# Weight loads in smaller pieces and later, loads limited to three under way, and the first batch routed two steps earlier, in a fused attention and mixture-of-depths kernel

## The chip, the cores and the metric

The kernel runs on one core of a Trainium2 chip. The metric is the device time of one execution in microseconds. Before the change it is 194.29 us, the median of three runs (193.64 to 196.32). A profile of one execution shows a span of 191.8 us, from the first to the last instruction.

The engines of a core run their own instruction streams and meet through semaphores: PE (matrix products; "PEld" is its loading of weights), DVE (vector work), ACT (copies out of the matrix memory and activations), POOL (further elementwise work, and the DMAs with row indices) and SP (issues plain loads). Data comes and goes through 16 DMA engines.

## The reference

Two stages, in 32-bit floating point. The first is linear attention with a decay per head, for 4 batches, 8 heads, 768 positions and a head size of 64, in blocks of 64 positions:

```python
for b in range(nb):
    intra = np.einsum('bhic,bhjc->bhij', qb, kb) * Dmask[None]
    intra = np.einsum('bhij,bhjd->bhid', intra, vb)
    inter = np.einsum('bhid,bhde->bhie', qb * lam_pow[None], kv_state)
    out[:, :, sl] = intra + inter
    kb_dec = kb * rev_pow[None]
    kv_state = lam_block[None, :, None, None] * kv_state + np.einsum('bhsd,bhse->bhde', kb_dec, vb)
```

The heads' outputs side by side give x of 768 tokens by 512 for each batch. The second stage gives each token a score, picks the 128 tokens of a batch with the highest scores, and adds a gated two-layer network to those alone:

```python
scores = np.einsum('bsd,d->bs', x, w_gate)
for b in range(B):
    top_idx = np.argpartition(-scores[b], capacity)[:capacity]
    xe = x[b, top_idx]
    h = np.maximum(xe @ w1, 0.0)
    ye = h @ w2
    g = 1.0 / (1.0 + np.exp(-scores[b, top_idx]))
    out[b, top_idx] = x[b, top_idx] + g[:, None] * ye
```

w1 is 512 x 1024 and w2 is 1024 x 512, 2 MB each.

## The kernel before

A *group* is 128 positions of one batch with all eight heads: two blocks of the reference. There are six groups in a batch (NT = 6) and 24 in all (NG = 24). The main loop (line 620) runs over groups; its pass g is called step g. It finishes group g and prepares groups g+1 and g+2. The order of the instructions on each engine is the order in which the program writes them (`manual_schedule`), so what a step writes first runs first on its engine.

The parts of a step, with their lines:

- `transposes(g+2)` turns queries and keys on PE (lines 199 and 210), and ACT copies them out (202, 216 or 219).
- `queries_decayed` and `keys_decayed` multiply by powers of the decay on POOL (224 and 187), giving qs and kd.
- `scores(g+1)` (line 237, PE) and `masked(g+1)` (244, DVE) give the block's masked scores p. `from_states(g+1)` (297) adds the share of the earlier blocks' state, which needs qs. `from_scores(g)` (308) multiplies p by the values; `outputs(g)` copies the result to x_b on ACT (322, 324) and stores it (334).
- `state_products(g+2)` (260, PE) gives keys times values. `next_state` adds them to the decayed state on DVE: either the decay is done first on POOL (`decay_state`, 270) and added (287), or both are folded into four DVE instructions (282).
- `gate_scores(g)` (347, DVE) gives the scores of the group's tokens. `row(g-1)` (370, PE) turns them into a row, and `compare(g-1)` and `compare_older` (376, 386, DVE) count for each token how many beat it.

When a batch is complete, `plan` (546) sets the steps of its second stage. `ranks` (422, 427, DVE) turns the counts into a 0/1 matrix "hit". `tokens` (438 on PE, 444 and 447 on DVE) makes the list of chosen tokens. `fetch` (461, POOL) gathers their rows from the output in memory into xs. `gate` (471 to 486) transposes xs and computes the gates. Then come 16 pieces on PE: eight `hidden` (499), each one eighth of the first layer, with a relu on ACT (504) after every four, and eight `back` (513), each one eighth of the second layer. After the last, DVE computes y (521) and POOL writes the rows back with an indirect DMA (525). The pieces are dealt out over steps by `counts`, so that PE has work in each. For the first batch: hit in step 6, tokens and fetch in step 8, gate in step 9, and four pieces in each of steps 9 to 12. For the second: hit, tokens and fetch in step 13, gate and pieces from step 15. The third runs into the end of the loop, and the fourth comes after it.

There are two forms of a step. The form for the start ("spare", steps below `SPARE` = 9) puts the transposes of g+2 first and folds one of the two state updates. The other (from step 9) puts the transposes late, uses half of the state products' bank for the transposed keys and lets POOL decay both states.

Loads are all issued by SP in program order: q, k and v of a group as three DMAs of 256 KB (line 69; runs of 64 elements, 256 bytes), six steps ahead (`AHEAD` = 6), into a ring of seven buffers (`AHEAD + 1`). A load waits until its buffer's last reader is done; nothing else holds it back. The weights stand in the same queue: w1 as four DMAs of 512 KB with runs of 1024 elements (4 KB, line 88) in step 2, w2 as four of 512 KB with runs of 2 KB (line 91) in steps 4 to 7:

```python
weights_at = [NT // 2 - 1] * NDC + [NT // 2 + 1 + i for i in range(NFC // 2)]
for g in range(NG):
    if g + AHEAD < NG:
        load(g + AHEAD)
```

The x_b of the second batch is not stored group by group but kept, and stored as two DMAs of 768 KB from step 12 on.

## Time and profile before

| | |
|---|---|
| time, median of 3 | 194.29 us |
| span of the profiled execution | 191.8 us |
| PE busy | 156.0 us (81%) |
| DVE / POOL / ACT busy | 112.7 / 94.2 / 68.3 us |
| loads on SP's queue (q1) | 76,544 packets, 23.07 MB |
| stores on ACT's queue (q10) | 3,538 packets, 6.30 MB |
| instruction fetches (q8) | 28 packets, 0.46 MB |
| q, k and v loads, issue to landing, median | 5.7 to 5.8 us |
| gather of xs, issue to landing, median | 4.6 us |

Two parts of the page show the span in 40 slices of 4.8 us, one digit for each, in tenths (9 is 90% or more): PEclk is the clock that PE was granted, DMA the busy share of the DMA engines.

```profile
PEclk9999999999669955999999969999999999999997
DMA  5999997899899999999879999411013211011001
```

The DMA engines are busy for the first 25 slices, about 120 us, and nearly idle after that. The clock of PE falls in three places: around 50, around 70 and around 108 us. A mean over the whole span hides this, so the kernel has to be read stage by stage. In the views of instructions in order of time, a line gives start, duration, engine, source line, operation, tiles (out<-in) and count, and in brackets the idle time of the engine before it with what ended it; "issue" means that it waited for nothing that the profile shows.

### The profile page before, as it was taken

The page shows a single profiled execution, that of the slowest core. Times are in us where ns is not written, and L with a number is a line of the kernel's source. Part 1 is how long each engine was busy: PE and PEld are TensorE (multiplying, and loading weights), DVE is VectorE, ACT ScalarE, POOL GpSimd, SP SyncE. Part 2 cuts the span into 40 slices and gives each one's busy share as a digit, 9 for nine tenths or more (in the row PEclk, how much of TensorE's full clock was granted, in tenths as well). Part 3 has the DMA queues.
Part 4 walks back from the last instruction along what each step waited for, and adds up shares of the span by engine and source line. Part 5 has one row for each costly group of instructions (what it writes and reads, how often), then busy time and mean ns, then how long its engine had stood idle before and what let it go on. Part 6 is the DMA issues. An engine that isn't in the chain of part 4 may idle for free.

```text
span 191.8 us, 8134 instructions
## 1 busy us (share of the span) xinstructions
PE 156.0 (81%) x3522; PEld 126.2 (66%) x3522; DVE 112.7 (59%) x382; ACT 68.3 (36%) x175; POOL 94.2 (49%) x102
## 2 busy tenths in 40 slices
PE   0897768685497459999996299999998988989990
PEld 0566657574486359996755299998666977539730
DVE  3813578589547423437698558767966889620000
ACT  2234545544055103344425055546244634111100
POOL 3358656736154525057448777676777610021002
PEclk9999999999669955999999969999999999999997
DMA  5999997899899999999879999411013211011001
GB/s 112 224 218 213 235 257 198 210 313 305 212 241 233 260 255 269 213 190 211 267 240 279 274 219 220 114 60 58 6 55 113 113 58 58 0 55 55 3 0 55
DMA packets 80757, 31.99 MB, mean 167 GB/s; under 512 B 75601, under 2 KB 75601, under 8 KB 80722
## 3 DMA queue, kind: packets, MB, share of 16 engines
q1 hardware_dynamic: 76544, 23.07, 54.7%
q10 hardware_dynamic: 3538, 6.30, 9.0%
q0 software_dynamic: 640, 2.10, 3.2%
q8 instruction: 28, 0.46, 1.1%
q14 instruction: 7, 0.06, 0.1%
HBM read 24.12 MB, written 7.34 MB: 164 GB/s over the span
## 4 chain that ended last, share of the span: by engine, by line
PE 43%; issue 15%; DVE 11%; DMA 7%; POOL 6%; ACT 3%; POOLq 1%; ACTq 0%; DVEq 0%
PE ph L499 9%; PE py L513 7%; PE po L308 5%; PE tq L199 5%; PE po L237 4%; PE pu L260 4%; DMA out_dram<-y,tok 4%; PE po L297 4%; DMA xs<-out_dram,tok 3%; ACT qT L202 3%; DVE cmp L386 2%; POOL qs L224 2%; DVE xg L347 2%; PE pu L210 2%; POOL decayed L270 2%
## 5 line engine op out<-in xcount | busy, mean ns | idle before, releaser
L270 POOL TENSOR_TENSOR decayed<-state,decay 128x256 f32<-128x256 f32 x32 | 28.5, 890 | 27.4 <-DVE state L282 12.3
L224 POOL TENSOR_TENSOR qs<-qT,qpow 128x512 f32<-128x512 f32 x24 | 30.8, 1282 | 20.8 <-ACT qT L202 19.2
L499 PE MATMUL ph<-xsT,w_sb 128*128 128x128 f32 x256 | 32.1, 285 | 0.7 <-ACT xsT L475 0.7
L499 PEld LDWEIGHTS ph<-xsT,w_sb 128*128 128x128 f32 x256 | 30.9, 200 | 1.1 <-ACT xsT L475 0.9
L386 DVE TENSOR_SCALAR_CACHE_REDUCE cmp<-sc_row,sc 128x128 bf16<-128x128 f32 (+3 forms) x66 | 29.9, 498 | 0.0
L187 POOL TENSOR_TENSOR kd<-kn,kpow 128x512 f32<-128x512 f32 x24 | 25.9, 1080 | 7.1 <-DMA kn<-in_k_dram 4.0
L513 PE MATMUL py<-w_sb,hs 128*128 128x512 f32 x64 | 29.2, 597 | 0.2 <-ACT qT L202 0.2
L202 ACT COPY qT<-tq 128x512 f32<-128x512 f32 x24 | 14.0, 584 | 39.3 <-PE tq L199 36.0
L237 PE MATMUL po<-qT,kT 64*64 64x64 f32 x768 | 18.7, 232 | 7.1 <-issue 6.4
L347 DVE CUSTOM_DVE_ANT_0 xg<-x_b,wg_b 128x512 f32<-128x512 f32 x24 | 24.2, 1007 | 0.0
L244 DVE TENSOR_TENSOR p<-po,mask 128x512 f32<-128x512 f32 x24 | 16.5, 688 | 12.9 <-PE po L297 12.8
L260 PE MATMUL pu<-vn,kd 64*64 64x64 f32 x704 | 19.6, 233 | 3.3 <-DVE state L287 3.3
L199 PE MATMUL tq<-ident,qn 128*128 128x128 f32 x96 | 17.6, 312 | 4.9 <-DMA qn<-in_q_dram 4.9
L237 PEld LDWEIGHTS po<-qT,kT 64*64 64x64 f32 x768 | 15.9, 146 | 8.2 <-issue 7.1
L308 PE MATMUL po<-vn,p 64*64 64x64 f32 x768 | 18.2, 232 | 3.3 <-issue 3.0
L308 PEld LDWEIGHTS po<-vn,p 64*64 64x64 f32 x768 | 14.5, 141 | 9.1 <-issue 5.8
L287 DVE TENSOR_TENSOR state<-pu,decayed 128x256 f32<-128x256 f32 x32 | 13.5, 420 | 11.7 <-ACT kT L219 7.6
L297 PE MATMUL po<-state,qs 64*64 64x64 f32 x704 | 18.1, 230 | 2.7 <-issue 1.5
L260 PEld LDWEIGHTS pu<-vn,kd 64*64 64x64 f32 x704 | 16.9, 147 | 5.1 <-issue 2.9
L513 PEld LDWEIGHTS py<-w_sb,hs 128*128 128x128 f32 x64 | 11.5, 191 | 11.4 <-issue 11.0
L376 DVE SCALAR_TENSOR_TENSOR cmp<-pb,sc,not_before 128x128 bf16<-128x128 f32 x22 | 7.7, 348 | 19.3 <-ACT sc_row L373 11.2
L297 PEld LDWEIGHTS po<-state,qs 64*64 64x64 f32 x704 | 15.6, 145 | 3.5 <-issue 2.1
(66 smaller groups left out, 170.3 us busy)
## 6 DMA issues: line engine op xcount, KB each, us to landing
qn<-in_q_dram SPq DMA_DIRECT2D x24, 256.0 KB, 5.8
kn<-in_k_dram SPq DMA_DIRECT2D x24, 256.0 KB, 5.7
vn<-in_v_dram SPq DMA_DIRECT2D x24, 256.0 KB, 5.7
out_dram<-x_b ACTq DMA_DIRECT2D x18, 256.0 KB, 4.3
w_sb<-in_moe_w_dram SPq DMA_DIRECT2D x8, 512.0 KB, 5.9
out_dram<-x_b ACTq DMA_DIRECT2D x2, 768.0 KB, 5.6
xs<-out_dram,tok POOLq DMA_INDIRECT x4, 4.6
out_dram<-y,tok POOLq DMA_INDIRECT x4, 3.1
```

Source lines behind the costliest of these rows:

```text
L187: nc.gpsimd.tensor_tensor(out=kd[:], in0=loaded[g][1][:], in1=kpow[:].rearrange("p a b -> p (a b)").unsqueeze(2).broadcast_to([128, H, D]) ...
L199: nc.tensor.transpose(tq[:, hp, :], in_=loaded[g][0][:, 2 * hp : 2 * hp + 2, :], identity=ident[:])
L224: nc.gpsimd.tensor_tensor(out=qs[:], in0=qTs[g][:], in1=qpow[:].rearrange("p a c i -> p a (c i)"), op=ALU.mult)
L237: nc.tensor.matmul(po[half[c], hh, 1, hp, :], lhsT=kT[half[hh], hp, half[c]], rhs=qT[half[hh], hp, half[c]], start=True, stop=True, skip_g ...
L260: nc.tensor.matmul(us[g][c][half[hh], hp * D : (hp + 1) * D], lhsT=kd[half[c], h, :], rhs=vn[half[c], h, :], start=True, stop=True, skip_g ...
L270: nc.gpsimd.tensor_tensor(out=t[:], in0=states[n][:], in1=decay[:], op=ALU.mult)
L297: nc.tensor.matmul(pos[g][half[hh ^ c], hh, 0, hp, :], lhsT=qs[half[hh], hp, half[c]], rhs=states[n][half[hh], hp, :], start=(hp == 0), st ...
L308: nc.tensor.matmul(pos[g][half[hh ^ c], hh, 0, hp, :], lhsT=p[half[c], hh, hp, :], rhs=vn[half[c], 2 * hp + hh, :], start=(hp == 0 and (2 ...
L347: nc.vector.tensor_tensor_reduce(out=xg[:], in0=x_bs[b][:, t].rearrange("p a b e -> p (a b e)"), in1=wg_b[:], scale=1.0, scalar=0.0, op0=A ...
L386: nc.vector.tensor_scalar(out=cmp[:, : cols.stop - cols.start], in0=rows_[b][:, cols], scalar1=scs[b][:, t : t + 1], scalar2=None, op0=op, ...
L499: nc.tensor.matmul(ph[:, fc % 4, :], lhsT=w1_sb[:, dc, fc * 128 : (fc + 1) * 128], rhs=keep["xsT"][:, dc, :], start=(dc == 0), stop=(dc == ...
L513: nc.tensor.matmul(py[:], lhsT=keep["hs"][:, fc, :], rhs=w2_sb[:, fc, :], start=(fc == 0), stop=(fc == NFC - 1),)
```

## The change

It has several parts:

- **Loads under way.** All loads go through `fetch_in`, which makes each of the first 31 loads (those of groups 0 to 8 and w1) wait on SP for the landing of the third load before it.
- **Three steps ahead.** `AHEAD` becomes 3. The ring keeps its seven buffers, so SP may still run ahead of the steps; what moves is the place of a load in the program, and with it the order among loads and weights.
- **Weights.** w1 comes behind group 8, as four DMAs of 512 KB, each a quarter of the columns with runs of 256 elements (1 KB). w2 comes as eight DMAs of 256 KB with runs of 1 KB, four behind group 10 and four behind group 11.
- **First batch earlier.** Its hit, tokens and fetch all come in step 6, its gate in step 7, its pieces as 3, 3, 3, 3, 2, 2 in steps 7 to 12. Its counting of older groups becomes part of `compare` again.
- **A third form of a step** for steps 6 to 11 (`g < FED`): transposes late, pieces before them, one state update folded. The start's form ends with step 5 (`SPARE` = 6).
- **The write of y** becomes a piece of its own, at the end of the step after the last `back`: step 13 for the first batch and step 21 for the second.
- The kept x_b of the second batch is stored from step 11 on.

It is meant to keep the queue of loads short while PE needs instructions and gathers through the same DMA engines, to have the weights there no earlier than needed, to give PE pieces earlier, and to take POOL's wait for y away.

The core of the diff:

```diff
-    AHEAD = 6
-    SPARE = NT + 3
+    AHEAD = 3
+    SPARE = NT
+    FED = 2 * NT
...
-    ld = ctx.enter_context(tc.tile_pool(name="ld", bufs=AHEAD + 1))
+    ld = ctx.enter_context(tc.tile_pool(name="ld", bufs=7))
...
+    def fetch_in(out, in_):
+        dma = nc.sync.dma_start(out=out, in_=in_)
+        if 3 <= len(issued) < 3 * (NT + 3) + F // 256:
+            tc.add_manual_dep(
+                dma.ins, issued[-3].ins.name,
+                mybir.DependencyInfo(mybir.DependencyClass.Sync, mybir.DependencyReason.DATA),
+                reason="loads under way",
+            )
+        issued.append(dma)
...
     def load_weights(i):
-        if i < NDC:
-            nc.sync.dma_start(out=w1_sb[:, i, :], in_=moe_w1[i * 128 : (i + 1) * 128, :])
+        if i < F // 256:
+            c, j, n, dst, src = i, 0, NDC, w1_sb, moe_w1
         else:
...
+            j, c = divmod(i - F // 256, HD // 256)
+            j, n, dst, src = 2 * j, 2, w2_sb, moe_w2
+        cols = slice(c * 256, (c + 1) * 256)
+        fetch_in(
+            dst[:, j : j + n, cols],
+            src[j * 128 : (j + n) * 128, cols].rearrange("(c p) e -> p c e", p=128),
+        )
...
-                nc.gpsimd.indirect_dma_start(
-                    out=rows_upto(b), out_offset=rows_at(), in_=y[:], in_offset=None,
-                )
+                keep["y"] = y
...
+        def write():
+            nc.gpsimd.indirect_dma_start(
+                out=rows_upto(b), out_offset=rows_at(), in_=keep["y"][:], in_offset=None,
+            )
...
-            ranked[s + 1 if b > 0 else s] = ranks
-            put(s + 1 if b > 0 else s + 2, 25, tokens)
+            at = s + 1 if b > 0 else s
+            ranked[at] = ranks
+            put(at, 25, tokens)
...
-            put(s + 2 if first else s + 1, 26, fetch)
-            gates[s + 3] = gate
+            put(s if first else s + 1, 26, fetch)
+            gates[s + 1 if first else s + 3] = gate
...
-            counts = [1, 2] if not whole else [4, 4, 4, 4] if first else [2, 3, 3, 3, 3, 2]
+            counts = [1, 2] if not whole else [3, 3, 3, 3, 2, 2] if first else [2, 3, 3, 3, 3, 2]
...
+            if step + 1 < NG:
+                writes.setdefault(step + 1, []).append(write)
...
-    weights_at = [NT // 2 - 1] * NDC + [NT // 2 + 1 + i for i in range(NFC // 2)]
+    n_w1, n_w2 = F // 256, NFC * HD // 512
+    weights_at = [NT + 2 - AHEAD] * n_w1 + [
+        NT + 4 - AHEAD + 2 * i // n_w2 for i in range(n_w2)
+    ]
...
-        if g >= 2 * NT and kept:
+        if g >= 2 * NT - 1 and kept:
...
+        elif g < FED and g + 3 < NG:
+            if g == NT:
+                for r in rows:
+                    row(r)
+            decay_state(2 * g + 4)
+            from_scores(g)
+            outputs(g)
+            scores(g + 1)
+            from_states(g + 1)
+            keys_decayed(g + 2)
+            if g == NT:
+                for r in rows:
+                    compare(r)
+                if g in ranked:
+                    ranked.pop(g)()
+            masked(g + 1)
+            if g in gates:
+                gates.pop(g)()
+            if g > NT:
+                in_order(pieces)
+            gate_scores(g)
+            start_u(g + 2)
+            transposes(g + 2)
+            state_products(g + 2)
+            next_state(2 * g + 4)
+            queries_decayed(g + 2)
+            if g != NT:
+                for r in rows:
+                    row(r)
+            next_state(2 * g + 5, fold=True)
+            if g == NT:
+                in_order(pieces)
+            else:
+                for r in rows:
+                    compare(r)
...
+        for write in writes.pop(g, []):
+            write()
```

## The prediction

> **What bounds the kernel now.** I read the busy time by stage first, then TensorE's (PE's) instructions in order of time with what ended each idle time, then GpSimd's (POOL's), then the DMA issues. The stages are cut at the first attention product (line 308) of steps 0, 6, 9, 10, 13, 16 and 23; columns: length, busy time of PE, its weight loads, VectorE (DVE), ScalarE, POOL, granted clock, DMA share, GB/s.
>
> ```profile
> 16.50:45.40 28.90, 21.81 (x791) 18.62 (x791) 19.97 (x72) 14.82 (x37) 18.08 (x20) 1.00 0.98 244
> 45.40:62.90 17.50, 12.11 (x411) 10.63 (x411) 11.79 (x49) 6.36 (x17) 8.00 (x9) 0.80 0.98 243
> 62.90:78.80 15.90, 11.37 (x161) 10.87 (x161) 4.88 (x15) 3.01 (x9) 6.58 (x6) 0.68 1.07 249
> 78.80:99.30 20.50, 20.21 (x444) 15.20 (x443) 13.60 (x46) 8.62 (x24) 10.69 (x10) 1.00 0.91 230
> 99.30:118.50 19.20, 14.21 (x422) 12.89 (x421) 13.59 (x36) 7.82 (x22) 13.26 (x14) 0.91 1.02 252
> 118.50:157.60 39.10, 37.87 (x991) 31.26 (x990) 30.70 (x98) 18.29 (x52) 25.71 (x25) 1.00 0.24 76
> 157.60:191.80 34.20, 27.45 (x180) 18.83 (x179) 10.56 (x42) 4.81 (x11) 3.17 (x3) 0.96 0.09 32
> ```
>
> PE is full at full clock from 78.8 to 99.3 and from 118.5 to 157.6: that time can't be shortened by moving work. The gains can only lie from 16.5 to 78.8 and from 99.3 to 118.5, where PE is idle for 7.1, 5.4, 4.5 and 5.0 us and its clock falls to 0.80, 0.68 and 0.91. In the first three DMA is busy all the time. PE there (start, duration, operation, idle time before it):
>
> ```profile
> 18.98 0.40 PE L297 MATMUL po<-state,qs 64*64 64x64 f32 x12 [1.07 <-issue]
> 38.00 0.39 PE L237 MATMUL po<-qT,kT 64*64 64x64 f32 x10 [1.05 <-issue]
> ...
> 45.92 0.41 PE L237 MATMUL po<-qT,kT 64*64 64x64 f32 x15
> 50.41 0.79 PE L237 MATMUL po<-qT,kT 64*64 64x64 f32 x17 [4.08 <-issue]
> ...
> 65.92 0.40 PE L308 MATMUL po<-vn,p 64*64 64x64 f32 x12 [2.48 <-issue]
> ...
> 70.94 1.12 PE L471 MATMUL pt<-ident,xs 128*128 128x128 f32 x4 [2.05 <-DMA xs<-out_dram,tok]
> ...
> 106.20 0.69 PE L297 MATMUL po<-state,qs 64*64 64x64 f32 x32 [1.22 <-POOL qs L224]
> 109.78 0.69 PE L260 MATMUL pu<-vn,kd 64*64 64x64 f32 x30 [2.79 <-DVE state L287]
> ```
>
> Four kinds of idle time. (a) Stops named "issue" in the middle of a group of products, on no semaphore. Counting matmuls and weight loads between one stop and the next gives 256 each time. The six in steps 0 to 5 are 1.07, 0.41, 0.45, 0.39, 1.05 and 0.46, sum 3.8 us. The 4.08 us one comes while the 512-KB pieces of w1, issued at 37.2 to 41.8, land. (b) The wait for the gathered rows xs at 70.94. (c) 106.20 and 109.78, behind POOL. (d) The half clock after each.
>
> POOL, which runs in order:
>
> ```profile
> 64.63 1.14 POOL L461 DMA_INDIRECT xs<-out_dram,tok  x1 [2.18 <-DVE state L282]
> 101.45 1.02 POOL L525 DMA_INDIRECT out_dram<-y,tok  x1 [3.40 <-DVE y L521]
> 107.76 1.00 POOL L461 DMA_INDIRECT xs<-out_dram,tok  x1 [0.47 <-issue]
> 108.75 0.15 POOL L365 MEMSET beaten<- 128x42 f32 x1
> 109.78 0.73 POOL L270 TENSOR_TENSOR decayed<-state,decay 128x256 f32<-128x256 f32 x1 [0.88 <-DVE state L287]
> 112.05 1.27 POOL L224 TENSOR_TENSOR qs<-qT,qpow 128x512 f32<-128x512 f32 x1 [0.54 <-ACT qT L202]
> ```
>
> The write of y holds POOL for 3.40 us, and kd, qs and decayed of the next groups stand behind it.
>
> **What the Trainium skill says.** "Runtime: NRT & Kernel Launch", Instruction fetch mechanics: an engine's instructions arrive in 16-KiB blocks of 256 instructions through a DMA queue, mostly hidden. The page's third part agrees (28 instruction packets, 0.46 MB) and so does the distance of 256 between stops; "mostly hidden" it is not, with 10.9 us of such stops by 66 us. "DMA: Bandwidth & Descriptors", Queues, rings and completion order: an engine serves its queues in turn, a packet at a time. By that a deep load queue would cost a block little; the 4.08 us stop behind 2 MB of w1 speaks for a longer wait than one packet. "TensorE: Matmul & The Clock Gate", Part 1: an idle window of about 3.4 us halves the clock until about as much busy time has passed. The trace agrees: after the 4.08 us stop the next four groups take 0.79 to 1.04 instead of 0.46 to 0.60 us.
>
> **The change part by part.** Times are of the start of a step's line-308 product: before, step 0 is at 16.5, 6 at 45.4, 9 at 62.9, 12 at 92.2, 13 at 99.3, 14 at 103.8, 16 at 118.5.
>
> *Three loads under way.* Each of the first 31 loads waits for the landing of the third before it. A load takes 5.1 to 6 us from issue to landing in the full queue, the lone last one 2.86. Loads land 1.18 us apart at the start, so three cover 3.5 us, enough for a 2.86 us round trip: I take the rate as kept. With the stores, group 8 lands at 40.8 in either. Behind SyncE's wait only other loads are queued. Without stops a step's chain is: line 308 0.62, scores and state products 1.0, p 0.6, state 0.41, gate score 0.72, two hand-overs 0.35, row transpose 0.29, about 4.05 us, against the measured 4.4 to 5.4. How much of the 3.8 us goes is not in the trace: between 0 and 3.8. The queue is a third shorter, and the small stops are the surplus of a fetch over a step, so I take 3.0: step 6 at 42.4.
>
> *w1 behind group 8, 1-KB packets, w2 as 8 issues of 256 KB.* Bytes are the same. w1 lands by about 49 (1.75 us for 512 KB before), group 9 by 53, w2's first half by 60, group 11 by 64, group 12 by 72; they are needed after 57, 60, 74, 74 and 80 (below). No cost. The long stop of step 6 loses its importance, for DVE sets that step.
>
> *Routing batch 0 in step 6.* DVE after row(5), by the durations at 45.2 to 50.2: row to hit 4.9, then p 0.75, gate score 0.76, state 0.42, folded state 0.85, token sum and cast 0.4, hand-over 0.3: the gather is issued 8.4 us after the row transpose. Gathers took 6.26, 5.05, 4.19 and 3.35 us to land, longest under full DMA; I take 5.7. So xs is there 13.85 us after step 6 begins, at 56.2. PE meanwhile does step 7's three attention groups and then waits some 6 us, as it did before in step 9, two steps later. From xs on: 5.0 us at full clock (pt 0.59, three hidden pieces 2.67, transposes 1.03, state products 0.47, row 0.25) plus 2.4 for the cold clock (7.6 against 5.2 us at 70.9 before), then steps 8, 9, 10 with three pieces at 5.84 each (6.73 with four, less 0.89), 0.8 in step 9 where the first w2 product follows the relu at once, and step 11 with two at 4.9: step 12 starts 30.6 us after xs, at 86.8. From step 6 to 12 that is 44.4 instead of 46.8 us. Gain so far 5.4.
>
> *Folded states in steps 6 to 11* put 0.43 us more on DVE and take 0.9 from POOL per step; PE's 5.84 hides both.
>
> *Steps 12 and 13.* DVE sets these: p, counts, scores, y, rank and hit run from 94.8 to 103.35 nearly without a gap, so two pieces fewer in step 12 bring nothing. Without POOL's 3.40 us wait for y about 0.2 is won net. Step 14 at 98.2.
>
> *The write of y a step later.* It now follows the gather of batch 1 on POOL, and the compiled order shows it waiting for that gather's landing: it writes what the gather reads. Behind it stand decayed, kd and qs of the next group, and PE's line 297 waits for qs. Before, the gather was issued 3.96 us after step 14 began and qs(16) ended 5.6 later. Now, with a gate score not slowed to 2.41 us by POOL beside it, the gather comes at 2.0; landing 5.05, issue of the write 1.1, decayed, kd, qs 3.0: qs at 11.2 against 9.5, and PE, idle for 3 us or more, restarts partly cold (0 to 2.1, I take 0.8, since the slow clock at 105 to 114 was there before). Loss 1.8, range 0 to 3.8.
>
> *Second write* moves to step 21, after its gather has long landed, and the tail is the same: 0.
>
> Sum: 3.0 + 2.4 + 0.2 - 1.8 = 3.8, so **190.5 us**.
>
> **The rivals.**
> 1. *Full gain* (0.30). All 3.8 us of stops go and the gather lands in 4.2 us as at 142.8, with a shorter cold stretch (2 instead of 2.4); the write costs nothing: 3.8 + 2.4 + 1.5 + 0.4 + 0.2 = 8.3, 186.0 us. For it: the stops come only where DMA is full. Against it: w2 and group 10 fill the queue when the gather runs.
> 2. *Won and lost* (0.15). The stops stay, since loads still fill DMA, and the write costs 3.8: 2.4 + 0.2 - 3.8 = -1.2, 195.5 us. For it: DMA share 0.98 would not change.
> 3. *Starved loads, slower* (0.13). With the 3.93 to 5.19 us of the first three loads as round trip, three under way give 1.5 us each, 4.5 a group and with the store 5.3: group 8 lands at 49 instead of 40.8, w1 and group 9 8 us later; steps 6 and 7 wait, step 6 at 48 (-2.6), xs no earlier than 62, write -3.8, other gains as in 2: 194.3 + 2.6 + 3.8 - 2.6 + 1.5 for a further cold stretch = 199.6 us. Against it: loads landed 1.2 us apart even at the start.
>
> **How the numbers follow.** The forecast has 0.42, the rivals 0.30, 0.15 and 0.13. The range is 184.5 to 197: from a little under rival 1 to above rival 2, leaving out rival 3 and the extremes. Two per cent below 194.3 is 190.4, which cuts the forecast in half: faster 0.30 + 0.22 = 0.52, same 0.20 + 0.15 = 0.35, slower 0.13.
>
> **What would show it.** The issue stops in steps 0 to 5 under 1 us in sum, and step 6 near 42.4. Group 8 landed near 41. DVE's hit about 5 us after row(5), pt about 14 us after step 6 begins with some 6 us of PE idle before it. Step 12 near 87. POOL's first write of y with some 4 us idle before it, ended by the gather's landing, and line 297 of step 15 waiting for qs. Wrong, if SyncE's waits spread the loads, if PE's stops stay, or if the gather in step 7 takes more than 7 us.

## The result and the profile after

The changed kernel takes 210.74 us, the median of four runs (207.81 to 211.74), beside 193.96 us for the kernel before on the same chip: a ratio of 1.09, 95% interval 1.064 to 1.117. It is slower by 17 us. The forecast was 190.5 us, range 184.5 to 197. The kernel before scatters by some 3 per cent from run to run (191.2 to 196.3 here, 188.6 to 200.1 over all the sets below), which limits what the smaller comparisons can say. A ratio and its interval are taken from the runs within 1.5 per cent of the fastest of each kernel, and so need not be the quotient of the medians beside them.

The profiled execution spans 209.1 us (191.8 before). The busy time by stage of the changed kernel, cut at the same steps as before (0, 6, 9, 10, 13, 16, 23), columns as before:

```profile
16.60:43.30 26.70, 19.76 (x788) 17.09 (x786) 21.37 (x72) 14.18 (x35) 18.04 (x19) 1.00 1.00 253
43.30:77.10 33.80, 22.82 (x473) 20.54 (x472) 12.74 (x49) 8.57 (x23) 10.70 (x11) 0.70 1.00 243
77.10:86.20 9.10, 6.44 (x140) 5.24 (x139) 3.19 (x12) 3.10 (x8) 2.83 (x3) 1.00 1.07 222
86.20:110.10 23.90, 18.19 (x410) 12.56 (x409) 13.06 (x44) 7.69 (x22) 10.09 (x11) 1.00 0.77 179
110.10:136.30 26.20, 15.85 (x424) 14.38 (x423) 16.03 (x46) 7.73 (x22) 15.16 (x16) 0.87 0.58 145
```

The first stage is 2.2 us shorter, as meant. A part of that is only the place of the cut: the transposes of group 8, eight products of about 1.1 us together, stood ahead of step 6's first product before and stand behind it now. The second stage is 16.3 us longer and the third 6.8 us shorter, since the wait for the gathered rows has moved from step 9 to step 7. The fourth stage, steps 10 to 12, is the surprise: PE's clock is full and it is still idle for 5.7 of 23.9 us, where before it was idle for 0.3 of 20.5. DMA is no longer full there (0.77). The fifth has 10.4 us of idle PE instead of 5.0.

PE of the changed kernel in order of time (start, duration, operation, idle time before it):

```profile
46.89 0.49 PE L254 MATMUL po<-qT,kT 64*64 64x64 f32 x8 [2.58 <-issue]
...
60.76 1.09 PE L488 MATMUL pt<-ident,xs 128*128 128x128 f32 x4 [6.02 <-DMA xs<-out_dram,tok]
62.53 4.81 PE L516 MATMUL ph<-xsT,w_sb 128*128 128x128 f32 x24 [0.68 <-ACT xsT L492]
...
80.75 0.27 PE L314 MATMUL po<-state,qs 64*64 64x64 f32 x1 [2.04 <-issue]
...
88.96 0.46 PE L314 MATMUL po<-state,qs 64*64 64x64 f32 x14 [1.21 <-issue]
...
93.68 0.92 PE L277 MATMUL pu<-vn,kd 64*64 64x64 f32 x32 [0.61 <-issue]
...
97.40 0.68 PE L314 MATMUL po<-state,qs 64*64 64x64 f32 x15 [1.41 <-issue]
...
105.02 0.69 PE L314 MATMUL po<-state,qs 64*64 64x64 f32 x31 [1.24 <-issue]
```

Lines 254, 277 and 314 are 237, 260 and 297 of the kernel before. Five things are to be seen. The wait for the gathered rows is 6.02 us long, as forecast, but by luck: counted from the beginning of step 6, the rows landed 3.5 us later than forecast, and PE came to them about as late. After the wait the 24 hidden products take 4.81 us at a granted clock of 0.59, and 2.94 us in the next step at 1.00: the cold clock. In steps 9 to 12 PE stops in the middle of line 314, on no semaphore: these are edges of instruction pages again (a *page* is a block of 256 of PE's instructions, fetched as one DMA packet), in steps 10 to 12 too, where the kernel before had no such stop. In each of steps 7 to 11 there is a wait of 0.61 us (0.89 once) ahead of line 277, which the kernel before does not have there: in the changed order the state products follow the transposes of k into the other half of the same tile `pu`. The trace puts no name to this wait, but it ends with ACT's copies of kT out of that tile: in step 10 the first of the two ends at 93.58 and line 277 begins at 93.68. And step 12's first product is at 102.58, not at 86.8.

```profile
93.20 0.66 ACT L236 COPY kT<-pu 128x256 f32<-128x256 f32 x2
```

Step 10 of the kernel before has neither a stop nor such a wait:

```profile
79.74 0.65 PE L297 MATMUL po<-state,qs 64*64 64x64 f32 x32
80.21 0.65 PE L260 MATMUL pu<-vn,kd 64*64 64x64 f32 x32
...
81.71 3.74 PE L499 MATMUL ph<-xsT,w_sb 128*128 128x128 f32 x32
```

POOL of the changed kernel where the first write of y stands:

```profile
117.80 1.00 POOL L478 DMA_INDIRECT xs<-out_dram,tok  x1 [0.15 <-issue]
...
125.33 1.01 POOL L546 DMA_INDIRECT out_dram<-y,tok  x1 [6.38 <-DMA xs<-out_dram,tok]
126.37 0.73 POOL L287 TENSOR_TENSOR decayed<-state,decay 128x256 f32<-128x256 f32 x1
127.05 1.04 POOL L204 TENSOR_TENSOR kd<-kn,kpow 128x512 f32<-128x512 f32 x1
128.05 1.26 POOL L241 TENSOR_TENSOR qs<-qT,qpow 128x512 f32<-128x512 f32 x1
```

The write waits 6.38 us for the landing of the gather before it, with decayed, kd and qs behind it; PE waits 6.52 us for that qs and starts again at 129.36. Before, the write held POOL for 3.40 us.

DVE of the changed kernel in step 6, ahead of the list of tokens that the first gather needs:

```profile
51.86 0.42 DVE L304 TENSOR_TENSOR state<-pu,decayed 128x256 f32<-128x256 f32 x1 [2.26 <-PE pu L277]
```

Where the 17.3 us of span went, by the start of steps: up to step 6, 2.1 won; steps 6 to 11, 59.3 against 46.8, 12.5 lost; steps 12 and 13, 1.7 lost; steps 14 and 15, 5.7 lost; the rest 0.5 won.

To read the stops I counted PE's matmuls and weight loads and matched every edge of 256 with the instruction packets in the trace. A packet is 16 KB and takes 0.9 to 1.5 us in most cases. It begins some time after PE *enters* the page ahead of it, and PE goes on 1.2 to 1.7 us after it has landed. So if the packet begins some 2 us after entry, a page must last 4 to 5 us to hide it. In the kernel before, the packet began 1.3 to 2.2 us after entry in steps 0 to 5, 5.8 behind w1. In the changed kernel, it began 0.2 to 1.1 us after entry in steps 0 to 4, 1.8 and 4.3 for the next two, and 5.6, 6.3, 5.1 and 4.4 us after entry for the four pages entered between 80.75 and 105.02. These times scatter from one execution to the next: in experiment 12, whose program is the changed kernel's up to step 7, the packets of steps 0 to 5 began 1.4 to 2.1 us after entry, as in the kernel before.

### The profile page after: what moved, and what is told of

The parts are those of the page before. It is cut to its first block, busy times and chain, and to the rows that moved or that the text cites. A ratio compares the mean times of both kernels' runs of the same rounds, so it can differ in the third digit from the quotient of the medians.

```text
span 209.1 us, 8155 instructions
## 1 busy us (share of the span) xinstructions
PE 158.8 (76%) x3522; PEld 127.5 (61%) x3522; DVE 113.6 (54%) x386; ACT 68.9 (33%) x178; POOL 92.7 (44%) x100
## 4 chain that ended last, share of the span: by engine, by line
PE 46%; issue 19%; POOL 10%; DMA 10%; DVE 10%; ACT 3%; POOLq 1%; ACTq 0%; DVEq 0%
PE ph L516 9%; PE py L530 9%; DMA xs<-out_dram,tok 6%; PE pu L277 5%; PE tq L216 4%; PE po L325 4%; PE po L314 4%; PE po L254 4%; POOL decayed L287 3%; POOL qs L241 3%; POOL kd L204 3%; DVE cmp L403 3%; PE pu L227 2%; DMA qn<-in_q_dram 2%; DVE xg L364 2%
## 5 line engine op out<-in xcount | busy, mean ns | idle before, releaser
L241 POOL TENSOR_TENSOR qs<-qT,qpow 128x512 f32<-128x512 f32 x24 | 31.6, 1316 | 44.8 <-ACT qT L219 43.2
L287 POOL TENSOR_TENSOR decayed<-state,decay 128x256 f32<-128x256 f32 x30 | 25.4, 846 | 24.5 <-DVE state L299 14.1
L516 PE MATMUL ph<-xsT,w_sb 128*128 128x128 f32 x256 | 33.3, 290 | 1.4 <-ACT xsT L492 1.4
L516 PEld LDWEIGHTS ph<-xsT,w_sb 128*128 128x128 f32 x256 | 31.8, 205 | 2.3 <-ACT xsT L492 2.0
L304 DVE TENSOR_TENSOR state<-pu,decayed 128x256 f32<-128x256 f32 x30 | 12.6, 421 | 34.5 <-PE pu L277 10.2
L403 DVE TENSOR_SCALAR_CACHE_REDUCE cmp<-sc_row,sc 128x128 bf16<-128x128 f32 (+4 forms) x65 | 29.8, 502 | 0.0
L277 PEld LDWEIGHTS pu<-vn,kd 64*64 64x64 f32 x704 | 17.1, 146 | 9.3 <-issue 6.5
L254 PE MATMUL po<-qT,kT 64*64 64x64 f32 x768 | 17.9, 229 | 5.3 <-issue 4.7
L254 PEld LDWEIGHTS po<-qT,kT 64*64 64x64 f32 x768 | 15.1, 143 | 6.3 <-issue 5.2
L341 ACT COPY x_b<-po 64x256 f32<-64x256 f32 x48 | 17.6, 366 | 0.6
L325 PE MATMUL po<-vn,p 64*64 64x64 f32 x768 | 17.1, 228 | 0.0
```

The lines of the kernel that those rows point to most:

```text
L241: nc.gpsimd.tensor_tensor(out=qs[:], in0=qTs[g][:], in1=qpow[:].rearrange("p a c i -> p a (c i)"), op=ALU.mult)
L254: nc.tensor.matmul(po[half[c], hh, 1, hp, :], lhsT=kT[half[hh], hp, half[c]], rhs=qT[half[hh], hp, half[c]], start=True, stop=True, skip_g ...
L277: nc.tensor.matmul(us[g][c][half[hh], hp * D : (hp + 1) * D], lhsT=kd[half[c], h, :], rhs=vn[half[c], h, :], start=True, stop=True, skip_g ...
L287: nc.gpsimd.tensor_tensor(out=t[:], in0=states[n][:], in1=decay[:], op=ALU.mult)
L325: nc.tensor.matmul(pos[g][half[hh ^ c], hh, 0, hp, :], lhsT=p[half[c], hh, hp, :], rhs=vn[half[c], 2 * hp + hh, :], start=(hp == 0 and (2 ...
L403: nc.vector.tensor_scalar(out=cmp[:, : cols.stop - cols.start], in0=rows_[b][:, cols], scalar1=scs[b][:, t : t + 1], scalar2=None, op0=op, ...
```

## The experiments

Each ran on the same chip as the kernel before, whose median there is given beside it. Kernel 1 is the kernel of experiment 1, and so on. Spans, step times and stops are those of one profiled execution; a step lasts from its first product to that of the next.

**1. State products ahead of the transposes**

```diff
             start_u(g + 2)
-            transposes(g + 2)
             state_products(g + 2)
+            transposes(g + 2)
             next_state(2 * g + 4)
```

> The changed kernel, with the state products of group g+2 written ahead of its transposes in steps 6 to 11, as the kernel before has them. In the changed kernel's trace the state products (line 277) of those steps start only after ACT has copied the transposed keys out of the same tile, 0.6 to 0.9 us after the transposes, and PE then stops again in the middle of line 314 for 1.2 to 2.0 us with no wait on record. Theory A (the new form of the step costs the time: the order makes PE wait for the copies, and the late state products also make the next page of instructions late): steps 8 to 11 take about 6 us with three pieces and 5 with two, the stops in steps 9 to 13 fall under 0.7 us each, and the time falls by 8 to 11 us, to about 200. Rival B (the stops come from the loads, which are unlimited from the 32nd on, with weights in 1-KB runs): the stops of 1.2 to 2.0 us stay, and only the wait for the copies goes, 3 to 5 us, to about 206. Rival C (the early routing costs: gather and cold clock in step 7): little changes, 208 or more.

Measured: 202.18 us beside 194.15, ratio 1.051 (1.037 to 1.064). 8.5 us of the 17 are gone. Steps 10 and 11 take 6.77 and 5.91 us (8.52 and 7.80 in the changed kernel), the waits before line 277 are gone, and of the stops in line 314 one is left, of 1.53 us in step 9. Behind it the 16 hidden products take 3.59 us instead of 2.05, so that step 9 takes 10.24 us (9.18 in the changed kernel). The packets of the four pages begin 1.6, 2.4, 1.0 and 3.0 us after entry. In the profiled run, of 204.6 us, steps 6 to 11, where the edit is, take 54.3 us instead of 59.3; another 3.2 us are won in steps 14 and 15, which it leaves as they are. Between experiments 2 and 3, which differ by the same edit, steps 6 to 11 go from 61.6 to 52.6 us. So the order inside a step was worth 5 to 9 us, about half of the loss; that the wait for the copies caused the late packets is not shown by this.

**2. Write of y one more step later**

```diff
-            if step + 1 < NG:
-                writes.setdefault(step + 1, []).append(write)
+            if step + 2 < NG:
+                writes.setdefault(step + 2, []).append(write)
```

> The changed kernel, with the write of y two steps after the last back piece instead of one, so step 14 for the first batch. In the changed kernel POOL waits 6.4 us in step 13 for the gather of the second batch to land before it can issue the write, and PE then 6.5 us for qs in step 15. Theory A (this wait is on the path and costs the 5.7 us by which steps 14 and 15 together grew, against the kernel before): the gap of PE before line 314 of step 15 goes, steps 14 and 15 together take 14 to 16 us instead of 20.5, and the time falls by 4 to 6 us, to about 205. Rival (the time of those steps comes from the gather and the routing as before, and the write only stands where PE waits anyway): less than 2 us.

Measured: 207.13 us beside 194.15, ratio 1.079 (1.069 to 1.089). Steps 14 and 15 take 12.3 us instead of 20.5 in its profile: PE's 6.5 us wait for qs is gone, as POOL shows, where decayed, kd and qs now run ahead of the write:

```profile
124.16 1.05 POOL L204 TENSOR_TENSOR kd<-kn,kpow 128x512 f32<-128x512 f32 x1
125.50 1.27 POOL L241 TENSOR_TENSOR qs<-qT,qpow 128x512 f32<-128x512 f32 x1 [0.30 <-ACT qT L219]
126.73 1.18 POOL L287 TENSOR_TENSOR decayed<-state,decay 128x256 f32<-128x256 f32 x1
129.08 1.04 POOL L546 DMA_INDIRECT out_dram<-y,tok  x1 [1.17 <-DMA xs<-out_dram,tok]
```

The total won only 3.6 us, since step 6 began 1.3 us later and steps 6 to 11 were 2.3 us longer in this execution (61.6 against 59.3).

**3. Both**

> Both edits at once: state products ahead of transposes in steps 6 to 11, and the write of y two steps later. If the two costs are independent, their gains add: 12 to 17 us, about 195, near the kernel before. If the routing of the first batch in step 6 is itself a loss, it stays above 198; if it is a gain as forecast, it is at or under 193.

Measured: 197.23 us beside 194.15, ratio 1.028 (1.016 to 1.040). The two account for 13.5 of the 17 us. What remains lies in steps 6 and 7, 23.9 us against 14.3 before: PE waits 5.58 us for the gathered rows there and runs on a cold clock after it. The other steps give back a part. The total lies between the two marks set for the early routing, above 198 for a loss and 193 for a gain.

**4. The limit of three loads alone, in the kernel before**

```diff
+    def fetch_in(out, in_):
+        dma = nc.sync.dma_start(out=out, in_=in_)
+        if 3 <= len(issued) < 3 * (NT + 3) + NDC:
+            tc.add_manual_dep(
+                dma.ins, issued[-3].ins.name,
+                mybir.DependencyInfo(mybir.DependencyClass.Sync, mybir.DependencyReason.DATA),
+                reason="loads under way",
+            )
+        issued.append(dma)
...
-            nc.sync.dma_start(out=t[:], in_=src[b, :, rows, :].rearrange("h p d -> p h d"))
+            fetch_in(t[:], src[b, :, rows, :].rearrange("h p d -> p h d"))
```

> The kernel before, with one part of the change alone: each of the first 31 loads waits for the landing of the third load before it (the order and the sizes of all loads stay). Theory (the limit keeps the queue short, so that the fetch of PE's next page of instructions waits less; the changed kernel shows 0.9 to 1.1 us from crossing a page to the fetch in steps 1 to 4, against 1.4 to 2.2 before): the six stops of steps 0 to 5, 3.8 us in sum, shrink to under 1.5, step 6 begins 1.5 to 2.5 us earlier, and the time is 1 to 3 us shorter, about 192. Rival (loads starve): step 6 begins later and the time is 196 or more. Rival (the chain of a step sets the pace and the stops lie beside it): step 6 within 0.5 us of before.

Measured: 191.47 us beside 194.15, ratio 0.998 (0.984 to 1.011). Step 6 begins at 43.5 instead of 45.4, and step 10 at 74.9 instead of 78.8; the total's interval includes no change. The stops of steps 0 to 5 came to 0.7 us in this profile, 3.8 before, as the theory has it. But kernel 7, with the same limit, has 3.3 us of such stops and begins step 6 at 43.5 as well. So step 6 comes 1 to 2 us earlier with the limit (43.3 to 43.5 in kernels 4, 7 and 10, against 44.4 and 45.4 in kernel 8 and the kernel before); that shorter stops are the reason is not shown.

**5. Products between transposes and state products.** Is it ACT's copies that hold the page back? Here state products still follow the transposes, but 2 to 5 us later.

```diff
-            if g > NT:
-                in_order(pieces)
-            gate_scores(g)
             start_u(g + 2)
             transposes(g + 2)
+            if g > NT:
+                in_order(pieces)
+            gate_scores(g)
             state_products(g + 2)
```

> The changed kernel with the hidden and back products of a step moved from ahead of the transposes to between the transposes and the state products; TensorE executes the same instructions, and the state products still come after the transposes, but 2 to 5 us later, so that ScalarE's copies of kT are long done when they begin. In the changed kernel steps 8 to 11 show 0.6 to 0.9 us of waiting ahead of the state products and 1.2 to 2.0 us stops in line 314 on a page of instructions whose fetch began only after that wait. Theory A (the wait for the copies is what holds the fetch back): both go, as in the kernel with the state products ahead: steps 10 and 11 at about 6.8 and 5.9 us, the fetches 1 to 3 us after their page is entered, about 202 us. Rival B (a page is fetched late for another reason, the reordering cured it by chance): the 0.6 us waits go and the line-314 stops stay: steps 10 and 11 near 8 and 7, about 207 us.

Measured: 203.09 us beside 196.17, ratio 1.034 (1.027 to 1.041). The total is near theory A's, but the profile is rival B's: steps 10 and 11 take 7.2 and 9.0 us. One of the four runs took 488.58 us, for a reason that is not known; it is not in the ratio. PE of this kernel:

```profile
76.33 0.68 PE L277 MATMUL pu<-vn,kd 64*64 64x64 f32 x16
...
79.54 0.46 PE L314 MATMUL po<-state,qs 64*64 64x64 f32 x16 [0.95 <-issue]
...
87.51 0.84 PE L314 MATMUL po<-state,qs 64*64 64x64 f32 x16 [1.94 <-POOL decayed L287]
```

The waits before line 277 are gone and two stops behind late packets stayed: the pages entered at 72.40, 79.54 and 87.41 had their successors begun 4.4, 5.5 and 4.5 us later. (The second stop is listed under POOL's decayed; it stands at a page's edge and ended 1.4 us after the packet landed.) So the wait for the copies costs its 0.6 us and does not hold the fetch back. The time won lies mostly elsewhere: steps 7 to 9 take 26.3 us instead of 34.3, the gather landed in 4.63 us instead of 6.81, and the hidden products of step 7 run at nearly the full clock (3.06 us), with the transposes ahead of them.

**6. The first gate one step later**, on kernel 3.

```diff
-            gates[s + 1 if first else s + 3] = gate
+            gates[s + 2 if first else s + 3] = gate
-            counts = [1, 2] if not whole else [3, 3, 3, 3, 2, 2] if first else [2, 3, 3, 3, 3, 2]
+            counts = [1, 2] if not whole else [4, 3, 3, 3, 3] if first else [2, 3, 3, 3, 3, 2]
...
-            at = s + 1 if first else s + 3
+            at = s + 2 if first else s + 3
```

> The kernel with state products ahead and the write two steps later (197.23), with gate and products of the first batch one step later (4, 3, 3, 3, 3 of them in steps 8 to 12); ranking, tokens and gather stay in step 6. Theory A (what is left of the loss is that only step 7's attention stands between the gather's issue and its use, so that TensorE waits 5.6 us and then runs 2 us slower on a cold clock): the gather still lands 10 us after step 6's tokens, but 3.5 us more work hides it; the wait shrinks to 1 to 3 us, steps 6 to 12 go from 52.6 to 47 or 48 us, the total to about 192. Rival B (the 6.8 us landing is the queue's doing and grows when w2 is under way, or the products are then the limit): the wait moves to step 8 unchanged, steps 6 to 12 stay at 52, the total at 197.

Measured: 192.84 us beside 196.17, ratio 0.985 (0.977 to 0.993). Theory A. The gathered rows landed at 57.31, before PE came to them: there is no wait for them at all, and steps 6 to 11 take 45.0 us instead of 52.6. PE of this kernel around the gate, line 488, which has no idle time before it:

```profile
59.23 0.85 PE L314 MATMUL po<-state,qs 64*64 64x64 f32 x32
60.01 0.66 PE L488 MATMUL pt<-ident,xs 128*128 128x128 f32 x4
61.34 3.84 PE L516 MATMUL ph<-xsT,w_sb 128*128 128x128 f32 x32 [0.68 <-ACT xsT L492]
```

**7. Kernel before, with limit and late write**: kernel 4, with the write of y a piece of its own as in the change, two steps after the last `back` as in experiment 2.

> The kernel before with three loads under way (191.5) and with the first write of y two steps after its last product, that is after the gather of the next batch has landed. Theory A (POOL's 3.4 us wait for y, with decayed, kd and qs behind it, makes the 2.8 and 1.2 us waits of TensorE in steps 13 to 15): steps 13 to 15 lose 2 to 4 us, total 187.5 to 189.5, faster than the kernel before by 2 to 3 per cent. Rival B (VectorE sets steps 12 to 15 anyway): no more than 0.5 us, total 191.

Measured: 189.13 us beside 196.17, ratio 0.966 (0.959 to 0.972): faster than both kernels. Steps 13 to 15 take 17.0 us (19.2 before).

**8. The weights alone, in the kernel before**

```diff
-        if i < NDC:
-            nc.sync.dma_start(out=w1_sb[:, i, :], in_=moe_w1[i * 128 : (i + 1) * 128, :])
...
+        cols = slice(c * 256, (c + 1) * 256)
+        nc.sync.dma_start(
+            out=dst[:, j : j + n, cols],
+            in_=src[j * 128 : (j + n) * 128, cols].rearrange("(c p) e -> p c e", p=128),
+        )
```

> The kernel before with only the weights' loads of the changed kernel: w1 in four 512-KB loads of 1-KB runs behind group 8, w2 in eight loads of 256 KB of 1-KB runs behind groups 10 and 11. Theory A (same bytes, same place: no cost): 193 to 195 us, groups 8 and later landing within 1 us of the kernel before. Rival B (runs of 1 KB take longer to move: 0.5 us or more per 512 KB, and shut out the fetches of instructions): the loads behind w1 land 3 us or more later, the gather of step 8 with them, 197 us or more. A shorter stop of step 6 (4.1 us behind w1's 4-KB runs before) would be a gain of 1 to 3 us that DVE may hide.

Measured: 192.95 us beside 196.17, ratio 0.980 (0.970 to 0.990). No loss, rather a gain. The packet behind w1 began 4.7 us after entry instead of 5.8, and the stop at that edge is 1.1 us shorter. That goes in the direction of what "DMA: Bandwidth & Descriptors", Queues, rings and completion order, of the Trainium skill says, an engine serving its queues in turn by packets: smaller packets ahead of it, a shorter wait. It does not show it: two executions of one program differ by more (experiments 13 and 14), and 4.7 us is still far more than one 1-KB packet's turn.

**9. The folded form in steps 6 and 7 alone**, on kernel 6.

```diff
-    FED = 2 * NT
+    FED = NT + 2
```

> The kernel with the first gate one step later (192.84), but with the folded states, the state products and transposes of the changed form only in steps 6 and 7; from step 8 on the late form of the kernel before. Theory A (the folded form costs where it ends, in step 12: two kd in a row on POOL, 1.7 us of TensorE waiting for kd, VectorE's hit 2.5 us late for step 13's tokens; steps 12 to 14 take 14.4 us there against 11.1 in the kernel before with limit and late write): that end moves to step 8, where TensorE waits for the gather or runs cold anyway; steps 12 to 14 take 11 to 12 us, total 189 to 190. Rival B (VectorE and POOL are as full in steps 12 to 14 in either form): 192 to 193.

Measured: 188.3 us beside 192.45, ratio 0.993 (0.985 to 1.002). Beside kernel 6, steps 12 and 13 take 12.2 us instead of 14.4, and PE's 1.70 us wait for kd in step 12 is gone; the wait of 2.45 us for hit in step 13 stayed. That speaks for theory A, but the ratio's interval, against the kernel before, includes no change, and in a second set of runs of the same kernel (number 14) these two steps took 14.0 us with a stop of 1.37 us at a page edge in step 12.

**10. Kernel 7 with the weights of the changed kernel**

> The kernel before with limit and late write (189.13), and the changed kernel's weights: w1 and w2 in 1-KB runs. Theory A (1-KB runs let the instruction fetches and group 9 through earlier: alone they gave 3 us, of which the shorter stop of step 6 was 1.1; with the limit that stop is already 1.5): 187 to 188.5. Rival B (both cure the same stop, so they don't add): 189 or a little more.

Measured: 191.82 us beside 192.45, ratio 1.013 (1.006 to 1.020). The gain of experiment 8 did not come again; number 7 had been 189.13 on another chip. In the profile the gather was issued at 63.9, beside the second four pieces of w2 (issued 60.8 to 63.2), instead of 60.8, and steps 6 to 11 took 48.6 us instead of 44.6. Nothing tells whether that is the weights' doing or the scatter.

**11. Pages shifted by half, from step 2**, in the changed kernel.

```diff
-        for hp, hh, c in quarters():
+        for hp, hh, c in [x for _ in range(3 if g == 4 else 1) for x in quarters()]:
```

> The changed kernel, with the 32 state products of one group in step 2 made three times over instead of once (same values in the same place): 128 more TensorE instructions, 1.3 us of work, which shifts every later page of 256 instructions by half a page. In the changed kernel the pages of steps 9 to 12 begin in or next to line 314, just ahead of the long expert products, and their successors are fetched 4.4 to 6.3 us later. Theory A (the place of the page's beginning in the step decides): the fetches of the pages entered between 80 and 110 us come 1 to 3 us after entry, the stops there (1.2 to 2.0 us each, 5.9 in sum) fall under 2 us in sum, total 206 to 208. Rival B (the order of state products and transposes, wherever the page begins): fetches still 4 to 6 us after entry, stops of the same sum on other lines, total 211 to 212.

Measured: 211.84 us beside 192.45, ratio 1.117 (1.106 to 1.127). Rival B's total, with neither's profile: steps 8 to 11 take 27.1 us instead of 32.7 and have no stop at an edge at all (packets 0.2 to 1.4 us after entry), and steps 2 to 5 take 27.5 us instead of 17.1, with stops of 1.94, 1.12, 3.18 and 1.69 us. A shift helped the later pages and harmed the early ones.

**12. The same shift from step 7 only**: line 254's products of group 8 three times over, in the gap where PE waits for xs.

> The changed kernel, with the score products of group 8 (line 254 of step 7) made three times over instead of once, in the place where TensorE waits about 6 us for xs: 128 more TensorE instructions that cost no time, and shift by half a page all pages after step 7 and none before. Theory A (the place in the step where a page of instructions begins decides whether the next one is fetched in time): steps 0 to 6 stay as in the changed kernel, the stops in line 314 of steps 9 to 12 (2.0, 1.2, 1.4, 1.2 us) are gone as they were with the shift in step 2, steps 9 to 12 begin 7 us apart instead of 8.5, total 204 to 206. Rival B (the shift in step 2 only traded stops, and the later steps were quick because less was in the load queue): 209 to 211.

Measured: 203.22 us (199.2 to 205.6) beside 196.6; the changed kernel was 210.74 (207.8 to 211.7). Adding 128 useless instructions made the kernel some 7 us faster. PE of this kernel in steps 9 and 10:

```profile
75.89 0.65 PE L314 MATMUL po<-state,qs 64*64 64x64 f32 x32
76.47 2.05 PE L516 MATMUL ph<-xsT,w_sb 128*128 128x128 f32 x16
...
80.92 0.68 PE L277 MATMUL pu<-vn,kd 64*64 64x64 f32 x16 [0.61 <-issue]
```

No stop in line 314, and the wait of 0.61 us before line 277 is still there in every step. The packets began 1.5, 1.2, 1.5 and 0.7 us after entry, where the changed kernel had 5.6, 6.3, 5.1 and 4.4. Steps 8 to 11 take 27.1 us instead of 32.7: these 5.6 us are the part of the gain that is the shift's in the profile. Another 1.6 us lie in step 6, ahead of the edit, and are scatter. Theory A for steps 8 to 11; but steps 0 to 5, whose program is the same, had stops of 3.8 us here and 0.6 us in the changed kernel.

**13. Kernel 9 with the weights of the kernel before**, and **14. kernel 9 again** on the same chip.

> The kernel with the folded form in steps 6 and 7 only (188.3), with the weights loaded as in the kernel before: w1 in 512-KB loads of 4-KB runs, w2 in four loads of 512 KB, one each behind groups 10 to 13. Theory A (the weights' packets matter by what they collide with; with the gather in step 6, the changed form keeps w1 from holding an instruction page and brings w2 in time): slower by 1 to 3 us, or even. Rival B (1-KB runs and the bunching of w2 cost 2.7 us, as the two kernels with the late gather read, 191.8 against 189.1): 2 to 3 us faster, about 186.

> The kernel with the folded form in steps 6 and 7 only, again, as the measure for the one with old weights on the same chip: 187 to 190, ratio to the kernel before 0.97 to 0.99.

Measured: 188.47 (186.8 to 189.9) and 191.34 us (189.6 to 193.6) beside 196.6. The old weights look 2.9 us better, but in the profiles the two begin step 12 only 0.4 us apart, and 1.8 us of the difference come after it, when no weights are loaded. There number 14 has a stop that number 9, the same program, does not have: both enter a page at 83.8 to 83.9, the packet of the next begins at 85.7 in one and at 88.7 in the other, and a stop of 1.37 us follows. So the scatter of the fetch alone makes a difference of that kind, and what the packets of the weights cost is not settled by these runs: within 3 us of nothing.

## Why the prediction was wrong, point by point

The step that failed is the length of steps 8 to 11: the forecast took it from PE's work alone, 23.2 us, and it was 32.7, since PE waited for ACT's copies in each of these steps and stopped at page edges in three of them. Two smaller terms failed beside it: the time until the gathered rows were used, and the size of the wait behind the write of y. In the order of the forecast's sum; its 190.5 us are a span of 188.0, by the 2.5 us between the time and the span of the kernel before:

- *Three loads under way: 3.0 us, step 6 at 42.4.* Somewhat less: step 6 at 43.27, 2.1 us won, of which the moved transposes are a part; 1.9 with the limit alone (experiment 4). The reason given, that the stops of 3.8 us go, is not shown: they came to 0.6 us in the changed kernel's profile, but to 3.8 us in experiment 12, whose program is the same there and which begins step 6 at 43.82. Where there were few stops, PE waited for DVE instead: it was idle for 7.1 us in this stage before and 6.9 after. Loads were not starved: group 8's last load landed at 40.0 (40.8 before). The rival that foresaw a slower kernel, starved loads, has the sign and not the mechanism: behind the first three, the loads of groups 1 to 8 landed after 2.9 to 4.8 us with three under way, and after 4.9 to 7.2 before.
- *xs 13.85 us after step 6 begins.* 17.4. The gather landed in 6.81 us rather than 5.7, and it was issued 10.8 us after the row transpose rather than 8.4: DVE's state sum, which stands ahead of the tokens' cast, waited 2.26 us for state products that came late behind a stop of 2.58 and the transposes. The path of DVE had been added up as if PE were never late.
- *5.0 + 2.4 us from xs to step 8.* 9.3. The cold clock was right in kind; 0.68 us of waiting for ACT's copy of xs and 0.61 ahead of line 277 were not in the sum. (That the clock halves after each kind of idle time was read too broadly: it was 1.00 over steps 0 to 5 of the kernel before, with six stops of 0.39 to 1.07 us.) "TensorE: Matmul & The Clock Gate", Part 1, of the Trainium skill, with its idle window of about 3.4 us, agrees: 24 products took 4.81 us after 6.02 us of idling, and 2.94 in the next step.
- *Steps 8 to 11 in 5.84 each, and 0.8 and 4.9: 23.2 us.* 32.7, the largest error, 9.4 us. "PE's 5.84 hides both" failed. PE's sum of work was about right, but I took it as the step's length. Three things were missing: the waits before line 277, 2.7 us in four steps (gone in 1 and 5), line 277 itself 0.92 us long instead of 0.69 behind two of them, and the stops at page edges in steps 9 to 11, 4.7 us. Together they make some 8 of the 9.4 us; the rest is not resolved. The prediction spoke of such stops as a matter of steps 0 to 6 alone, where DMA is full. Experiment 12 shows that the stops go when the edges are moved in the step, and 1 that most of them go with another order of state products and transposes and the same number of instructions. "Runtime: NRT & Kernel Launch", Instruction fetch mechanics, has the blocks of 256 instructions, which fits; its "mostly hidden" was wrong in the kernel before and is so again here.
- *Steps 12 and 13: 0.2 won.* 1.7 lost. A stop of 1.24 us at an edge in step 12, and the change of form there was not costed: POOL makes two kd in a row (2.04 us), and PE waits 0.32 us for them behind the stop, 1.70 us in kernels 1 and 6, where no stop stands before.
- *The write of y: 1.8 lost, 0 to 3.8.* The mechanism is the forecast one, line by line, with the size off: steps 14 and 15 took 20.5 us against 14.7, 5.7 lost. The gather was issued 1.96 us after step 14 began, as forecast (2.0); the landing took 6.72 us instead of 5.05, and 0.81 us more passed until the write began, so qs ended 13.5 us after the step's beginning, not 11.2. The sum itself was loose: its own terms, 1.7 us for the later qs and 0.8 for the restart, make 2.5 and not 1.8. The rest of the 3.9 us is the restart, line 314 at 1.14 us with the clock at 0.87 over the stage, and short waits around it. Experiment 2 took 8.2 us out of these steps.
- *Weights: no cost.* Not contradicted, and not settled to better than 3 us (8, 10, 13, 14).
- *Second write and tail: 0.* Right: 0.5 us the other way.

From 188.0, the forecast as a span, the errors are 0.9 in the first steps, 3.5 at xs, 1.9 up to step 8, 9.4 in steps 8 to 11, 1.9 in steps 12 and 13, 3.9 in steps 14 and 15, and -0.5 after: 21.0, and 209.1 was measured.

Routing the first batch early is not what costs: kernels 9, 13 and 14 keep the early ranking and gather and are faster than the changed kernel by 19 to 22 us. What cost in it is the use of the rows in step 7, behind one step's attention alone: one step later, in experiment 6, steps 6 to 11 took 7.6 us less. Nor is the early routing shown to gain: steps 6 to 11 take 44.7 us in kernel 9 and 44.6 in kernel 7, which routes as before. PE is busy for 38.8 us of them in kernel 9, at a mean clock of 0.81, and for 34.6 us in kernel 7, at 0.89: less idle time, but a colder clock.

What stays open is why the packet of a page begins late. It isn't the load queue alone: in the changed kernel the DMA engines moved nothing from 92 to 95 us while the packet of the page entered at 88.96 began only at 95.21. It isn't the wait for the copies (5 and 12). And it differs between executions of one program (9 and 14), so that the place of an edge alone does not settle it either.

## What to carry to other kernels

Before forecasting a reordered step as the sum of its busiest engine, mark the edges of its instruction pages and each new pair of writer and reader in a tile: here, 256 instructions that run in under 5 us left no room for a fetch that began 2 us late, and two halves of one tile were one dependency. A gather with row indices took up to 7 us here, and needs as much other work on the engine that waits for its rows; an indirect write behind it on the same queue held up the work behind that for as long. Where 5 to 7 us of a loss vanish with a shift of the instructions by half a page, that part is not the algorithm's. And compare the same steps in more than one execution before naming a cause: stops of 0.6 and 3.8 us came from one and the same piece of program.

## What the runs showed of the hardware that was not expected

- Adding 128 instructions that compute nothing new, in idle time, made the kernel 7 us faster (203.2 against 210.7); 5.6 us of it lie in steps 8 to 11, where the page edges had moved and the stops were gone.
- The time from entering a page to the start of the next one's fetch was 0.2 to 6.3 us, and not only under full DMA; PE resumed 1.2 to 1.7 us after the packet landed. In the same program it was 1.8 us in one execution and 4.7 in another, and the stops of steps 0 to 5 came to 0.6 us in one and 3.8 in another.
- With three loads under way instead of all, loads landed after 2.9 to 4.8 us instead of 4.9 to 7.2, with the last of group 8 there at 40.0 us instead of 40.8.
- The gather of 128 rows took 3.3 to 3.4 us at the end with little else under way, 3.3 to 4.4 for the third batch, and 4.2 to 7.1 for the first two, beside loads and stores.
